# Turning q in 64x64 pieces instead of 64x128 for four of the attention groups

## The chip, the cores and the metric

The kernel runs on one NeuronCore of a Trainium2 chip. The metric is the device time of one execution in microseconds, lower is better; the time before is 195.84 us, the median of three runs.

## What is computed

Two layers in a row, on batch 8, 8 heads, 576 positions, head width 64 (so 512 columns), all inputs and the output in float32:

```python
# attention without a score matrix
q_s = softmax(q, axis=-1)            # over the 64 columns of a head
k_s = softmax(k, axis=2)             # over the 576 positions
kv  = einsum('bhsd,bhse->bhde', k_s, v)
x   = einsum('bhsd,bhde->bhse', q_s, kv)   # then heads side by side: [B, 576, 512]
# channel mix, D = 512, d_ff = 1024
x_prev = x shifted by one position, zero in front
xk = mu_k * x + (1 - mu_k) * x_prev
xr = mu_r * x + (1 - mu_r) * x_prev
k  = relu(xk @ w_k);  v = (k * k) @ w_v
out = sigmoid(xr @ w_r) * v
```

## The kernel before

**Work by group.** The attention works on 16 groups, two for each batch element b: a group (b, g) holds four heads: heads 2g and 2g+1 on partitions 0 to 63 and 64 to 127 (`r` in the code), and the heads four further on beside them in the columns (`u`). A head's 576 positions are J = 9 blocks of 64, and block j holds every ninth position. Groups (0,0) and (0,1) fold mu into the weights of X and go another way through X; they are not touched.

**Steps of a group**, by the names that the order uses (tag bg): `load` brings q, k and v by DMA; ScalarE (ACT) makes `expq`, `expk` and casts v (`cast`); VectorE (DVE) makes `rsum`, `rrec` and `scale`, which leaves the softmax of q in a tile `qs`. TensorE (PE) turns q (`T`, line 371: each 64-position block against a 64x64 identity, the result in bf16 in a PSUM pair `att_a` or `att_b`), and forms the product of k and v with the sums of k in one more column (`KV`, line 401). DVE makes the reciprocal of those sums (`rz`, line 408) and the scaled weights (`w`, line 418); ACT copies the turned q to SBUF (`qt`, line 379). Then PE multiplies both (`X`, line 541). ACT copies x out of PSUM (`xb` for the first 512 positions, `xs` for the last 64), and DVE makes the shifted copy's edge (`edge`, line 557), the difference (`diff`), the two scaled differences (`sc`, line 566) and xk and xr (`mix`, line 571).

**Blocks on PE.** For b of 1 and more one recorded operation holds several of these: `TKVbg` is T and KV, `Bbg` is the X of the group before, then T, then KV. A group in `CROSSBAR` (b of 5 and more) has its q turned by a transposing DMA and has no T. X of a few groups stands by itself (`ALONE`).

**How T is cut.** For each block of 64 positions and each half `r` of the partitions, T makes either one transpose of 64 rows by 128 columns (both `u` at once, the result on 128 PSUM partitions), or two of 64 by 64 (one for each `u`, each with its own 64 PSUM partitions). The tuple `WHOLE` lists the groups that take the first form: 18 transposes and 18 weight loads instead of 36 and 36. Before the change these are both groups of batches 0 and 1 and the first groups of batches 2 and 3. Groups (2,1), (3,1), (4,0) and (4,1) take the second form.

**Channel mix.** It runs in ten units of up to 512 positions: `k` (line 637, into PSUM banks mm_a to mm_d), `relu` on ACT, `sq` on DVE, `r` (line 673) with `th` on ACT, `v` (line 693), then `o` on DVE (line 699), which reads the bank of v and frees it, then the store.

**Order.** Nothing is scheduled at run time: the string `ORDER` lists all operations by hand-fixed name, with the buffer that each takes, and every engine runs its own in that sequence. Semaphores alone decide when. DMAs of loads and weights are issued by GpSimd (POOL) and, at the start and for stores, by SyncE (SP). The order around the change is

```
... k14 ... T of (1,0) in TKV10 -> r02 r01 r00 r03 -> B11 -> v0x -> X11 -> v0x -> k1x -> TKV20
-> r10 r11 k14 r12 r13 -> B21 -> v1x -> X21 -> v1x -> r20 -> TKV30 -> v13 -> k2x -> B31 ...
```

Of the kernel before, what the change touches and what calls it, by code (L numbers as in the profile page):

```python
# [32 lines left out]
XO = 368  # L33

FILLS = 27
WHOLE = ((0, 0), (0, 1), (1, 0), (1, 1), (2, 0), (3, 0))
FUSED = ((0, 0), (0, 1))
EARLY_UNITS = 2
SPLIT = ((1, 1),)
# [144 lines left out]
def graph(kn):  # L184
# [135 lines left out]
    def attention(b, g):  # L320
# [46 lines left out]
        def transpose_q(slot):  # L367
            for j in range(J):
                for u in ((slice(0, 128),) if (b, g) in WHOLE else two):
                    for r in range(2):  # L370
# [500 lines left out]
```

## Time and profile before

| | |
|---|---|
| median of three runs | 195.84 us (195.44 to 196.55) |
| the profiled execution | 195.36 us, of which 193.6 us are the span of the instructions |
| PE busy | 185.6 us, 96% of the span |
| DVE, ACT, POOL busy | 153.0, 138.8 and 41.4 us |
| granted TensorE clock | 0.998 on average |
| from HBM, to HBM | 33.56 MB, 9.44 MB |
| line 371 | 252 transposes (108 of 64x128, 144 of 64x64), each with a weight load, from 10.3 to 86.1 us |

Times of instructions count from the start of the span. A row of the timeline has the start, the time from there to the last end of the merged instructions, the engine, the line, the operation, its tiles as output<-inputs, and the shapes; for PE "64*128" says how many rows and columns of the array are in use. In brackets stands the idle time of the engine ahead of it and what ended it; idle times below 0.15 us are not listed. Matmuls overlap in PE's pipeline, so their starts, not their durations, show how long they hold it. Busy time of PE therefore can hide short waits.

### The profile page before, as it was taken

Reading aid. Unit: us, or ns where it says so; the run is one execution under the profiler, and the core shown is the slowest. Engines: PE = TensorE matmul, PEld = TensorE weight load, DVE = VectorE, ACT = ScalarE, POOL = GpSimd, SP = SyncE. Lnnn points to the kernel's source line nnn. Section 1 sums busy time; section 2 is a strip of 40 time slices with the busy share of each in tenths; the row PEclk is TensorE's granted clock in tenths of the full one; section 3 lists DMA queues with packets and bytes.
Section 4 is the critical chain, followed back from the end, with each engine's and each line's share of the span. In section 5 each row is a group of like instructions: output and inputs, shape, how many; then the busy total and the mean of one; then the engine's idle time right before and its main releaser. Section 6 shows DMA issues by size and latency. Waiting matters only on the chain.

```text
span 193.6 us, 4658 instructions
## 1 busy us (share of the span) xinstructions
PE 185.6 (96%) x1830; PEld 90.1 (47%) x1830; DVE 153.0 (79%) x355; ACT 138.8 (72%) x219; POOL 41.4 (21%) x65
## 2 busy tenths in 40 slices
PE   7988979999999999999999999999999999999991
PEld 2364434444535544654544444444444444444751
DVE  1899874999999999999999999988966863242531
ACT  3777999899999999898999798653754235421440
POOL 8345557554225114320210000000000000000000
PEclk9999999999999999999999999999999999999999
DMA  6999999999999999997793371449014145024813
GB/s 182 316 314 254 328 330 246 405 390 401 410 392 402 402 415 358 360 383 282 130 297 119 85 166 27 64 105 183 1 25 106 36 108 135 0 54 110 190 30 108
DMA packets 23614, 41.86 MB, mean 216 GB/s; under 512 B 9372, under 2 KB 12712, under 8 KB 23592
## 3 DMA queue, kind: packets, MB, share of 16 engines
q0 software_dynamic: 9392, 27.99, 43.9%
q1 hardware_dynamic: 13384, 12.14, 24.7%
q10 hardware_dynamic: 816, 1.44, 2.3%
q8 instruction: 14, 0.23, 0.5%
q14 instruction: 8, 0.07, 0.1%
HBM read 33.56 MB, written 9.44 MB: 222 GB/s over the span
## 4 chain that ended last, share of the span: by engine, by line
PE 84%; DMA 11%; POOL 2%; issue 0%; DVE 0%; POOLq 0%
PE mm_d L693 10%; PE mm_b L693 9%; PE mm_a L637 8%; PE mm_c L637 7%; PE mm_b L637 7%; PE mm_c L693 7%; PE mm_a L693 7%; DMA wk_ab<-in_moe_w_k_dram 7%; PE mm_d L637 6%; PE mm_c L673 5%; PE mm_d L673 5%; DMA wr<-in_moe_w_r_dram 4%; PE mm_a L673 4%; PE mm_b L673 3%; PE att_b L541 1%; PE att_a L541 1%
## 5 line engine op out<-in xcount | busy, mean ns | idle before, releaser
L693 PEld LDWEIGHTS <-k_a 128*128 128x128 bf16 x160 | 15.4, 98 | 18.5 <-issue 0.6
L673 PEld LDWEIGHTS <-xr 128*128 128x128 bf16 x144 | 13.6, 98 | 16.8 <-DMA wr<-in_moe_w_r_dram 1.5
L693 PEld LDWEIGHTS <-k_b 128*128 128x128 bf16 x136 | 12.9, 98 | 13.8 <-issue 0.4
L637 PEld LDWEIGHTS <-wk_ab 128*128 128x128 bf16 x80 | 7.8, 98 | 8.5 <-issue 0.5
L673 PE MATMUL mm_c<-wr,xr 128*128 128x512 bf16 x40 | 10.3, 380 | 1.4 <-DMA wr<-in_moe_w_r_dram 1.4
L637 PEld LDWEIGHTS <-wk_bb 128*128 128x128 bf16 x80 | 7.8, 98 | 7.7
L637 PEld LDWEIGHTS <-wk_aa 128*128 128x128 bf16 x80 | 7.6, 98 | 8.2 <-issue 0.8
L637 PEld LDWEIGHTS <-wk_ba 128*128 128x128 bf16 x80 | 7.5, 98 | 8.1 <-issue 0.5
L673 PE MATMUL mm_d<-wr,xr 128*128 128x512 bf16 x40 | 10.3, 379 | 0.0
L673 PE MATMUL mm_a<-wr,xr 128*128 128x512 bf16 x36 | 9.3, 380 | 0.0
L624 ACT ACTIVATE rel_a<-mm_b 128x512 bf16<-128x512 f32 (+1 forms) x7 | 3.6, 508 | 7.3 <-PE mm_b L637 7.1
L628 DVE TENSOR_TENSOR k_a<-rel_a 128x512 bf16<-128x512 bf16 x14 | 5.9, 421 | 3.1 <-ACT rel_a L624 2.9
L624 ACT ACTIVATE rel_c<-mm_a 128x512 bf16<-128x512 f32 (+1 forms) x11 | 6.1, 556 | 3.1 <-PE mm_a L637 2.8
L637 PE MATMUL mm_c<-xk,wk_ab 128*128 128x512 bf16 (+1 forms) x26 | 7.5, 362 | 0.6 <-ACT xk L501 0.6
L637 PE MATMUL mm_c<-xk,wk_aa 128*128 128x512 bf16 (+1 forms) x26 | 7.3, 363 | 0.0
L628 DVE TENSOR_TENSOR k_a<-rel_c 128x512 bf16<-128x512 bf16 x14 | 5.8, 417 | 1.7 <-ACT rel_c L624 1.7
L673 PE MATMUL mm_b<-wr,xr 128*128 128x512 bf16 x28 | 7.2, 379 | 0.0
L637 PE MATMUL mm_a<-xk,wk_ba 128*128 128x512 bf16 (+1 forms) x24 | 6.9, 371 | 0.0
L637 PE MATMUL mm_a<-xk,wk_bb 128*128 128x512 bf16 (+1 forms) x24 | 6.9, 370 | 0.0
L637 PE MATMUL mm_b<-xk,wk_aa 128*128 128x512 bf16 (+1 forms) x24 | 6.5, 353 | 0.0
L637 PE MATMUL mm_b<-xk,wk_ab 128*128 128x512 bf16 (+1 forms) x24 | 6.5, 352 | 0.0
L624 ACT ACTIVATE rel_a<-mm_c 128x512 bf16<-128x512 f32 x7 | 4.2, 602 | 3.2 <-PE mm_c L637 1.7
(344 smaller groups left out, 542.8 us busy)
## 6 DMA issues: line engine op xcount, KB each, us to landing
raw_k<-in_q_dram POOLq DMA_DIRECT2D x3, 576.0 KB, 8.4
raw_e<-in_k_dram POOLq DMA_DIRECT2D x3, 576.0 KB, 11.0
raw_f<-in_v_dram POOLq DMA_DIRECT2D x3, 576.0 KB, 6.5
out_dram<-th_a SPq DMA_DIRECT2D x13, 128.0 KB, 3.0
out_dram<-th_f SPq DMA_DIRECT2D x12, 128.0 KB, 2.4
out_dram<-th_b SPq DMA_DIRECT2D x10, 128.0 KB, 4.6
out_dram<-th_c SPq DMA_DIRECT2D x10, 128.0 KB, 2.4
raw_a<-in_q_dram POOLq DMA_DIRECT2D x2, 576.0 KB, 9.9
```

The lines of the kernel that those rows point to most:

```text
L541: kn.nc.tensor.matmul(kn.half(slot, u)[two[r], to:to + n], lhsT=kn.ws[w.index][two[u], r, :], rhs=x_columns(r, u, at, n), start=True, stop ...
L624: kn.nc.scalar.activation(out=kn.rels[rel.index][:, 0:n], in_=kn.bank(kf)[:, 0:n], func=ACT.Relu, scale=HALF_ROOT)
L628: kn.nc.vector.tensor_tensor(out=kn.k2s[k2.index][:, fc, 0:n], in0=kn.rels[rel.index][:, 0:n], in1=kn.rels[rel.index][:, 0:n], op=ALU.mult)
L637: kn.nc.tensor.matmul(kn.bank(kf)[:, 0:n], lhsT=kn.wk[fc // 4][ct % 2][:, ct // 2, (fc % 4) * 128: (fc % 4) * 128 + 128], rhs=kn.xs[0][:, ...
L673: kn.nc.tensor.matmul(kn.bank(rps), lhsT=kn.xs[1][:, ct, c:c + 128], rhs=kn.wr[:, ct, :], start=(ct == 0), stop=(ct == CT - 1))
L693: kn.nc.tensor.matmul(kn.bank(vps)[:, 0:width], lhsT=kn.k2s[k2.index][:, ft, 128 * m:128 * m + 128], rhs=wv_of(ft)[:, part], start=(ft == ...
```

## The change

`WHOLE` loses four groups: (1,0), (1,1), (2,0) and (3,0). Their q is turned by 36 transposes of 64x64 in place of 18 of 64x128. `ORDER` stays as it is, the other engines run the same instructions in the same sequence, and the PSUM columns and partitions that are written stay the same.

```diff
 FILLS = 27
-WHOLE = ((0, 0), (0, 1), (1, 0), (1, 1), (2, 0), (3, 0))
+WHOLE = ((0, 0), (0, 1))
 FUSED = ((0, 0), (0, 1))
```

The loop that reads it (unchanged):

```python
for j in range(J):
    for u in ((slice(0, 128),) if (b, g) in WHOLE else two):
        for r in range(2):
            kn.nc.tensor.transpose(
                out=turned(slot, r)[u, 64 * j:64 * j + 64],
                in_=kn.qss[qs.index][two[r], j, u],
                identity=kn.ident[two[r], two[r]])
```

## Prediction

> **What bounds the kernel now.** I read the page first. Its first section says that PE is busy 96% of the span, and the granted clock is 9 tenths or more in every slice:
>
> ```profile
> PE 185.6 (96%) x1830; PEld 90.1 (47%) x1830; DVE 153.0 (79%) x355; ACT 138.8 (72%) x219; POOL 41.4 (21%) x65
> ```
>
> Next the waits of PE. Five are long enough to be listed, 3.9 us together, and all lie before 27 us. The longest is the one that matters here:
>
> ```profile
> PE mm_c L673 <- DMA wr<-in_moe_w_r_dram: 1.4, 1, 1.4
> ```
>
> By these two views PE sets the end, and PE time saved after 27 us should come off the end. So I read PE's timeline at the blocks in question: first column the start, then the time until the last end, both in us. The blocks are B11 (30.48 to 31.64), TKV20 (45.43 to 46.21) and, for comparison, B21 (50.63 to 51.62), which has the 64x64 form already:
>
> ```profile
> 30.48 0.22 PE L541 MATMUL att_a<-qt_c,w_a 64*64 64x64 bf16 x4
> ...
> 30.86 0.44 PE L371 MATMUL att_a<-ident,qs_a 64*128 64x64 bf16 x18
> 31.23 0.48 PE L401 MATMUL att_a<-vv_b,ek_a 64*64 64x65 bf16 x36
> 31.64 0.60 PE L693 MATMUL mm_d<-wv_a,k_a 128*128 128x512 bf16 x2
> ...
> 45.43 0.44 PE L371 MATMUL att_a<-ident,qs_b 64*128 64x64 bf16 x18
> 45.80 0.48 PE L401 MATMUL att_a<-vv_c,ek_b 64*64 64x65 bf16 x36
> 46.21 1.04 PE L673 MATMUL mm_c<-wr,xr 128*128 128x512 bf16 x4
> ...
> 50.63 0.22 PE L541 MATMUL att_b<-qt_b,w_c 64*64 64x64 bf16 x4
> ...
> 50.90 0.48 PE L371 MATMUL att_b<-ident,qs_c 64*64 64x64 bf16 x36
> 51.20 0.49 PE L401 MATMUL att_b<-vv_a,ek_c 64*64 64x65 bf16 x36
> 51.62 0.60 PE L693 MATMUL mm_a<-wv_a,k_b 128*128 128x512 bf16 x2
> ```
>
> Starts are what counts, since matmuls overlap. 18 transposes of 64x128 hold PE for 0.37 us, 36 of 64x64 for 0.30. Twice the instructions take less time, because PE runs four 64x64 ones beside each other and two 64x128 ones (8 ns and 21 ns from start to start, on the whole).
>
> Then I asked whether PE really waits for nobody after 27 us. The list leaves out short gaps, so I read the timeline of all engines where PE reuses PSUM banks that VectorE (DVE) has to empty:
>
> ```profile
> 31.77 0.17 DVE L408 RECIPROCAL rz_a<-att_a 128x2 f32<-128x2 f32 x1 [2.35 <-PE att_a L401]
> ...
> 33.03 0.43 DVE L557 COPY xb_a<-xb_a 128x126 bf16<-128x126 bf16 x1
> ...
> 40.16 0.68 DVE L699 SCALAR_TENSOR_TENSOR th_b<-th_b,mm_d 128x512 f32<-128x512 f32 x1
> 40.33 0.59 PE L637 MATMUL mm_a<-xk,wk_ab 128*128 128x512 bf16 x2
> 40.90 0.59 PE L637 MATMUL mm_d<-xk,wk_ba 128*128 128x512 bf16 x2
> 42.02 0.67 DVE L699 SCALAR_TENSOR_TENSOR th_c<-th_c,mm_b 128x512 f32<-128x512 f32 x1
> 42.19 0.59 PE L637 MATMUL mm_c<-xk,wk_ab 128*128 128x512 bf16 x2
> 42.75 0.59 PE L637 MATMUL mm_b<-xk,wk_aa 128*128 128x512 bf16 x2
> ```
>
> Two 512-column matmuls take 0.43 us from start to start in the rows around. From 40.33 to 40.90 it is 0.57, from 42.19 to 42.75 it is 0.56. In both places PE starts 0.06 us after DVE has emptied the bank it needs (40.16 + 0.68 = 40.84, and 42.02 + 0.67 = 42.69). So PE lost 0.14 and 0.13 us to DVE, and the "busy" PE hid it. The busy time by stage (length, PE, PEld, DVE, ACT) tells who is really short:
>
> ```profile
> 24.00:33.00 9.00, 7.56 (x143) 3.76 (x142) 5.20 (x13) 9.00 (x17) 6.04 (x9) 1.00 1.18 278
> 33.00:43.00 10.00, 10.00 (x53) 4.22 (x52) 9.90 (x23) 8.71 (x12) 5.01 (x8) 1.00 1.04 395
> 43.00:62.00 19.00, 19.00 (x270) 9.13 (x269) 18.86 (x39) 18.77 (x27) 7.71 (x11) 1.00 1.04 400
> ```
>
> From 24 to 33 us ACT has no gap. From 33 to 62 us DVE has none but its own hand-overs (9.90 of 10, 18.86 of 19), and from 62 to 72 it is busy 10.00 of 10.00. PE is timed by them and is merely full as well.
>
> **The change, part by part.** Four groups get 36 transposes in place of 18, with as many weight loads. No other engine's order moves, and no wait is added. PSUM banks, columns and partitions written are the same, so the copies qt behind them cost what they do now.
>
> B11: it becomes what B21 is. From the first X matmul to the next big matmul 31.64 - 30.48 = 1.16 us now, 51.62 - 50.63 = 0.99 then: -0.17. Of this 0.11 is the step from X to T (30.86 - 30.48 = 0.38 against 50.90 - 50.63 = 0.27), since PE no longer passes from one tile shape to another there, and 0.06 the transposes.
>
> TKV20 and TKV30: no X ahead, so a shape change stays in front. Now 46.21 - 45.43 = 0.78 (TKV30: 59.02 - 58.24 = 0.78). Then 0.30 + 0.42 (T and KV in B21) = 0.72: -0.06 each. Split transposes straight behind a 128-row matmul are not in the trace. KV bounds that: straight behind a shape change it took 46.21 - 45.80 = 0.41, without one 0.42, so nothing extra; 0.05 extra is the other end (the first transposes of TKV20 behind a shape change run no slower than that). A gap of PE's own is possible too: KV of B41 took 86.60 - 86.11 = 0.49 against 0.42 in the other split blocks, with no wait shown; so +0.07 a block is the upper end. I take -0.06.
>
> TKV10: 0 at any price up to about 1.4 us, because PE waits 1.44 us behind it for the weights wr (26.93). If that cover went, it would be -0.06 as well.
>
> PE's own sum is -0.17 - 0.06 - 0.06 = -0.29 us. Now what of it reaches the end. The time that B11 gives is met at 40.90 and 42.75, where DVE decides. Would DVE be earlier? It waits 2.35 us for B11 at 31.77, but only for rz11 and w11; two squares follow, and then it stands at edge10 (33.03), which needs xs10 and xb10 from ACT. ACT starts xb10 at 31.80, straight behind th02, in its stretch without a gap, and of B11 it needs only the X matmuls ahead of T. So edge10 stays at 33.03 and so does everything that DVE does in sequence behind it: the 0.17 turns into longer waits at 40.90 and 42.75. From 42.75 on PE is where it was. TKV20 and TKV30 give 0.12 by 59 us; at 61.62 PE uses mm_b again 0.06 us after DVE is done with it (60.88 + 0.68 = 61.56), next to nothing to spare, and at 68.99 a weight load of r30 stands 0.06 us behind DVE's xr (68.18 + 0.75) and is listed with that releaser: DVE decides there too. DVE has no gap from 33.03 to there, so it cannot be earlier. After 69 us all is as before.
>
> So: -0.29 on PE, of which 0.27 to 0.29 turns into waits for DVE; change of the end 0.00, at most -0.02. The profiled execution took 195.36 us, 193.6 of it the span and 1.76 around it; it would be 195.36 again. The median of the three runs is 195.84, 0.48 above it, and that is where I put the changed kernel: **195.8 us**.
>
> One rule speaks against the change. The Trainium skill, TensorEngine Tiling (Restrictions and Gotchas), says that column tiling excludes the fast weight load, and TensorE: Matmul & The Clock Gate (LDWEIGHTS; Weight-path perf modes) gives fast loads to 128 columns alone and 1/1.2 ns per column to the others. An estimate from the second page is 53 ns for each 64-column load, 1.9 us for 36 if they come one after another, some +1.5 us in each of TKV20 and TKV30. The sum by it would be +3.0, so 198.8. The trace agrees that these loads are longer (108 ns on average against 95 for the 64x128 ones at L371) and disagrees that this costs anything in B21, where 36 loads and transposes pass in 0.30 us.
>
> **The rivals.**
> 1. *PE's gain reaches the end*: -0.29, so 195.55. For it: PE 96% and the chain of waits, which is PE from 26.93 on. Against it: the two gaps above and a DVE without gaps. It would still be within 0.5%, which is 0.98 us and about what a measurement of this kernel can tell from no change.
> 2. *Slower: the weight loads stand in a row*. The place is T20 and T30, where no X has put PE into the 64x64 shape. If the loads there came one by one at the 108 ns that L371's 64x64 loads last, T would take 36 x 0.108 = 3.9 us in place of 0.37, both together +7.0, so 202.8; PE would pass DVE as the bound, as there is no more than some 0.04 us of waiting to eat up behind them. It decides from (0.98 + 0.12 + 0.04)/72 = 16 ns extra for each transpose, 24 ns in place of 8. Against it: 8 ns in all four split blocks of this trace (B21, B31, B40, B41), though each has an X ahead.
> 3. *Slower by little*: PE's own gaps of 0.07 in three blocks, +0.2 less the gain; nothing visible, within 0.5%.
> That the change does not do what it says is no rival: the built program has four runs of 18 more transposes and nothing else.
>
> **How the numbers follow.** Forecast (DVE takes the gain) 0.62; rival 1 0.15; rival 3 0.06; all three within 0.5%, 0.83. Rival 2 past its point 0.09, and 0.03 for the spread of the runs (195.44 to 196.55 is 0.57% alone): slower 0.12. Faster by over 0.98 us has no mechanism, since even the whole of PE's sum is 0.29; 0.05 for the spread and what I do not see. The range goes from the lowest run less rival 1, 195.44 - 0.29 = 195.15, to the highest run, 196.6; only rival 2 and the far ends lie outside.
>
> **What would show it.** Right: T at B11, TKV20, TKV30 with x36 and 0.30 us to KV; B11 0.99 us long; the gap at 40.90 about 0.14 longer or the wait at 42.75 in its place; DVE's edge10 at 33.03 and all PE starts after 69 us where they are now. Wrong: PE starts after 69 us earlier by 0.1 or more (rival 1: then DVE had room that I did not see); T20 or T30 longer than 0.45 us (rival 2); a DVE instruction between 33 and 69 us that moves.

## The result: slower, by a pause inside one block

| | before | changed |
|---|---|---|
| median | 195.25 us (195.0 to 197.28) | 196.41 us (195.93 to 197.91) |
| ratio | 1 | 1.0065, 95% interval 1.005 to 1.008 |
| profiled execution | 195.36 us, span 193.6 | 196.10 us, span 194.2 |

Both medians are of 18 runs taken beside each other, so the loss is 196.41 - 195.25 = 1.16 us. The median of before that the prediction used, 195.84, was that of three of these runs, and lies 0.59 us above that of all 18.

The page of the changed kernel:

```profile
PE 185.5 (95%) x1902; PEld 90.1 (46%) x1902; DVE 152.9 (79%) x355; ACT 138.7 (71%) x219; POOL 41.4 (21%) x65
...
q8 instruction: 15, 0.25, 0.5%
```

144 more instructions on PE (72 matmuls, 72 weight loads), and PE busy no longer than it was (185.5 against 185.6 us). The loss is therefore idle time of PE. Its list of waits has a row of a kind that before did not have in this stage, "issue", which means that PE waited for no semaphore that the profile shows:

```profile
PE mm_c L673 <- DMA wr<-in_moe_w_r_dram: 1.3, 1, 1.3
...
PE att_b L401 <- issue: 0.6, 1, 0.6
```

PE's timeline of the changed kernel (start, time to the last end) at the blocks that the prediction named, then at B40, the block of group (4,0), whose own instructions the change does not touch:

```profile
30.29 0.22 PE L541 MATMUL att_a<-qt_c,w_a 64*64 64x64 bf16 x4
...
31.27 0.60 PE L693 MATMUL mm_d<-wv_a,k_a 128*128 128x512 bf16 x2
...
39.12 0.38 PE L637 MATMUL mm_c<-xk,wk_ab 128*128 128x512 bf16 x1
39.48 0.59 PE L637 MATMUL mm_a<-xk,wk_aa 128*128 128x512 bf16 x2
40.13 0.59 PE L637 MATMUL mm_a<-xk,wk_ab 128*128 128x512 bf16 x2
40.73 0.59 PE L637 MATMUL mm_d<-xk,wk_ba 128*128 128x512 bf16 x2
...
42.02 0.59 PE L637 MATMUL mm_c<-xk,wk_ab 128*128 128x512 bf16 x2
42.58 0.59 PE L637 MATMUL mm_b<-xk,wk_aa 128*128 128x512 bf16 x2
...
45.26 0.48 PE L371 MATMUL att_a<-ident,qs_b 64*64 64x64 bf16 x36
45.57 0.47 PE L401 MATMUL att_a<-vv_c,ek_b 64*64 64x65 bf16 x36
45.97 1.04 PE L673 MATMUL mm_c<-wr,xr 128*128 128x512 bf16 x4
...
60.88 0.59 PE L637 MATMUL mm_a<-xk,wk_ab 128*128 128x512 bf16 x2
61.44 0.59 PE L637 MATMUL mm_b<-xk,wk_aa 128*128 128x512 bf16 x2
...
70.51 0.22 PE L541 MATMUL att_b<-qt_b,w_c 64*64 64x64 bf16 x4
...
70.78 0.48 PE L371 MATMUL att_b<-ident,qs_c 64*64 64x64 bf16 x36
71.08 0.45 PE L401 MATMUL att_b<-vv_a,ek_c 64*64 64x65 bf16 x31
72.16 0.23 PE L401 MATMUL att_b<-vv_a,ek_c 64*64 64x65 bf16 x5 [0.64 <-issue]
72.32 1.04 PE L673 MATMUL mm_a<-wr,xr 128*128 128x512 bf16 x4
```

VectorE's rows in the same trace, just ahead of three of these places:

```profile
32.95 0.35 DVE L557 COPY xb_a<-xb_a 128x126 bf16<-128x126 bf16 x1 [0.38 <-ACT xb_a L552]
38.76 0.67 DVE L699 SCALAR_TENSOR_TENSOR th_a<-th_a,mm_a 128x512 f32<-128x512 f32 x1
60.71 0.67 DVE L699 SCALAR_TENSOR_TENSOR th_b<-th_b,mm_b 128x512 f32<-128x512 f32 x1
```

And the rows of before that belong beside them, at mm_b near 61 us and at KV of B40:

```profile
61.19 0.59 PE L637 MATMUL mm_a<-xk,wk_ab 128*128 128x512 bf16 x2
61.62 0.59 PE L637 MATMUL mm_b<-xk,wk_aa 128*128 128x512 bf16 x2
...
71.17 0.49 PE L401 MATMUL att_b<-vv_a,ek_c 64*64 64x65 bf16 x36
```

Three readings. First, the parts that were changed did what was forecast: B11 takes 31.27 - 30.29 = 0.98 us, TKV20 45.97 - 45.26 = 0.71. Second, VectorE took the gain: a matmul that used to follow after 0.22 us starts 0.36 us after the one before it at 39.48, the gap at 40.73 is 0.60, and at 61.44 there is one of 0.56 where before had 0.43. At 39.48 and 61.44 PE starts 0.05 and 0.06 us after VectorE has emptied the bank that it needs (38.76 + 0.67 = 39.43, and 60.71 + 0.67 = 61.38). Third, in KV of B40 the 32nd of 36 matmuls does not come. The 31st starts at 71.33, the next at 72.16: a pause of 0.83 us in the middle of a row of equal instructions, none of which waits for a semaphore. Before has the 36 in one row.

### The profile page after: what moved, and what is told of

It is laid out like the page before. It is cut to its first block, busy times and chain, and to the rows that moved or that the text cites. A ratio compares the mean times of both kernels' runs of the same rounds, so it can differ in the third digit from the quotient of the medians.

```text
span 194.2 us, 4802 instructions
## 1 busy us (share of the span) xinstructions
PE 185.5 (95%) x1902; PEld 90.1 (46%) x1902; DVE 152.9 (79%) x355; ACT 138.7 (71%) x219; POOL 41.4 (21%) x65
## 3 DMA queue, kind: packets, MB, share of 16 engines
q10 hardware_dynamic: 816, 1.44, 2.3%
## 4 chain that ended last, share of the span: by engine, by line
PE 84%; DMA 11%; POOL 2%; issue 1%; DVE 0%; POOLq 0%
PE mm_d L693 10%; PE mm_b L693 9%; PE mm_a L637 8%; PE mm_c L637 7%; PE mm_b L637 7%; PE mm_c L693 7%; PE mm_a L693 7%; DMA wk_ab<-in_moe_w_k_dram 7%; PE mm_d L637 6%; PE mm_c L673 5%; PE mm_d L673 4%; DMA wr<-in_moe_w_r_dram 4%; PE mm_a L673 4%; PE mm_b L673 3%; PE att_b L541 1%; PE att_a L541 1%
```

## What the pause is: theories

The page counts DMA packets by queue. The instruction queue q8 carries 14 packets of 16384 bytes before and 15 now, with PE's own instructions up from 3671 to 3815 recorded ones. The line of before:

```profile
q8 instruction: 14, 0.23, 0.5%
```

In the trace's packets one of them lies just ahead of the pause: it starts at 69.68 us and lands at 70.78. The DMA view of that stretch alone has it:

```profile
q8 instruction: 1, 0.02, 5.8%
```

**Theory 1 (pages).** PE's program comes in pages by DMA. PE has passed the last instruction of one page and the next is not usable yet. In the changed kernel a pause of 0.56 us also ends at 16.82 (hidden, since PE waits for wr later), and between it and the pause in B40 PE ran 767 matmuls with their weight loads, 1535 instructions with one that only waits: six times 256, but for one. So a page is taken to be 256 instructions, and counting on in steps of 256 gives every other border. The two pauses end 1.27 and 1.38 us after a page has landed. In this stage a page's transfer starts 2.15 to 3.58 us after PE has reached the border before it, 3.29 us after for this one. (Elsewhere in the runs some start as much as 1.8 us ahead of that border.) Two borders that PE reaches 4.94 us apart (66.39 us in B31, 71.33 in B40) are then too close: 3.29 to the start, 1.10 to land, 1.38 to be used make 5.77, and 5.77 - 4.94 = 0.83. This sum splits the measured time into its parts; it must come out, and tests nothing. The experiments have to. The Trainium skill, Runtime: NRT & Kernel Launch (Instruction fetch mechanics), says that the program is refilled in blocks of 16 KiB, 256 instructions, and that crossing a border costs one tail-bump, "mostly hidden"; the trace agrees with the size, and here the cost is not hidden.

By this theory nothing is wrong with split transposes. They only add 144 instructions ahead of B40, so every border behind them falls 144 instructions earlier in the work. Before, the same stretch had its borders at 63.13 (among big matmuls), 70.94 and 83.93.

**Theory 2 (cost of each split T).** The four groups cost about 0.3 us each somewhere (their loads, shape changes, or a late effect of them).

A further question: did VectorE really take PE's gain, as forecast?

## The experiments

Ratios are to the kernel before on the same chip, with their 95% intervals; "border" is a border of 256 PE instructions.

**1. One group fewer, (3,0).**
```diff
-WHOLE = ((0, 0), (0, 1))
+WHOLE = ((0, 0), (0, 1), (3, 0))
```


> The changed kernel with group (3,0) left at 18 transposes of 64x128; (1,0), (1,1) and (2,0) split. Theory 1 (PE's program comes in pages of 16384 B, 256 instructions; the page border that falls into KV of block B40 comes only 5 us after the border before it, and the page is not there yet): 36 instructions fewer ahead of B40 move that border behind the block, to a matmul near 74 us, 7.7 us after the border before. No pause in B40 (KV there 0.29 to 0.35 us from first to last start, not 1.1); time ratio to before 0.998 to 1.002. Theory 2 (each split T costs by itself, 0.3 us a group): three quarters of the loss stay, ratio 1.004 to 1.006.

Measured 1.0017 (1.0006 to 1.0029), and no pause in B40:

```profile
71.31 0.49 PE L401 MATMUL att_b<-vv_a,ek_c 64*64 64x65 bf16 x36
```

Three of four splits are in, and three quarters of the loss are not. The page that was late now lands 3.18 us ahead of its border, which PE reaches at 74.55.

**2. One group fewer, (1,0)**, the one whose T lies under the wait for wr.
```diff
+WHOLE = ((0, 0), (0, 1), (1, 0))
```


> The changed kernel with group (1,0) left at 18 transposes of 64x128; (1,1), (2,0) and (3,0) split. Theory 1 (pages): the number of PE instructions ahead of B40 is the same as with (3,0) left whole, so the border falls behind B40 again: no pause there, ratio 0.998 to 1.002, although another group is the one left whole. Theory 2 (cost of each split T): T of (1,0) is covered by PE's wait for wr, so leaving it whole gives nothing back: ratio 1.006.

Measured 1.0014 (0.9995 to 1.0033); KV of B40 again 36 in one row. Which group stays whole does not matter for the pause, only the count. Theory 2 at 0.3 us a group falls with these two: from the first r matmul behind wr to the last matmul of the kernel the two profiles need 162.48 and 162.45 us, before 162.48. The ratios of experiments 1, 2 and 4 (1.0014 to 1.0019, two of the intervals wholly above 1) leave 0.3 us or so that these stretches do not show in 1 and 2; that rest is open.

**3. Before, with 72 idle pairs.** An idle pair is a weight load and a matmul on zeros, whose result nobody reads. No T is changed.
```diff
+    pad_slot = Slot("mm")
+...
+        for i in range(72):
+            kn.nc.tensor.matmul(kn.bank(pad_slot)[two[i % 2], 0:64], lhsT=kn.still[0:64, 0:64],
+                                rhs=kn.still[0:64, 64:128], start=True, stop=True)
```

(In place of "..." stands the head of the function; `ORDER` has the operation as `pad:2`, just ahead of r02, in PSUM bank mm_c.)

> The kernel before, all its T as they were, with 72 pairs of a 64x64 weight load and a 64-column matmul on a zeroed tile put in front of r02, where PE waits 1.4 us for the weights wr: the same 144 PE instructions more as in the change, none of them a transpose, and about 1 us of PE time that the wait covers. Theory 1 (pages): the borders stand at B31 and B40 exactly as in the changed kernel, so KV of B40 pauses by 0.5 to 1.2 us and the ratio is 1.003 to 1.007. Theory 2 (cost of each split T): no T is split, ratio 0.999 to 1.001.

Measured 1.0079 (1.0065 to 1.0094), a little above the expected end. The pause sits behind the same instruction, the 31st matmul of KV in B40:

```profile
71.36 0.45 PE L411 MATMUL att_b<-vv_a,ek_c 64*64 64x65 bf16 x31
72.74 0.23 PE L411 MATMUL att_b<-vv_a,ek_c 64*64 64x65 bf16 x5 [0.93 <-issue]
```

(Lines are ten further on.) The page had landed at 71.38, 1.36 us before PE went on. The loss of the change is here without the change.

**4. Another block made shorter: (4,0) whole, all four splits in.**
```diff
+WHOLE = ((0, 0), (0, 1), (4, 0))
```


> The changed kernel, all four groups split, with group (4,0), which was split before as well, turned by 18 transposes of 64x128. Theory 1 (pages): block B40 is 36 instructions shorter, the border that fell into it comes after it: no pause; the whole T costs PE 0.16 us in that block. Ratio 0.999 to 1.002. Theory 2 (cost of each split T, as in the change): the four splits stay, ratio 1.005 to 1.008.

Measured 1.0019 (1.0007 to 1.003). B40 has no pause. KV of TKV20 and TKV30 took 0.11 us longer than in the changed kernel, by a pause of 0.12 and 0.11 us at no border; why is open.

**5 and 6. Less DMA traffic.** The changed kernel and the one before, with the loads of q, k and v of batches 4 to 7 cut to 64 of 576 columns. Both kernels leave out the rest of that input and compute on old data. (At the second "..." the destination of the load is narrowed in the same way.)
```diff
+        n_cols = 64 if b >= 4 else J * D
 ...
-                             ap=[[J * D, 128], [4 * S * D, u.stop - u.start], [1, J * D]])
+                             ap=[[J * D, 128], [4 * S * D, u.stop - u.start], [1, n_cols]])
 ...
```


> The changed kernel, with the loads of q, k and v of batches 4 to 7 cut to 64 of the 576 columns of each row (the rest of the raw tiles keeps old data; it leaves out eight ninths of that input). PE's instructions and the page borders are those of the changed kernel. Theory 1 with a late page (the page is late because its transfer starts 3.3 us after it is due, behind the input loads that keep the DMA engines full until 76 us): the transfer now starts within 1.5 us of the border in B31, and KV of B40 has no pause (0.29 to 0.35 us). Theory 1 without that part (the page is late for another reason, its own length or PE's speed): the pause of 0.5 us or more stays. Theory 2 (cost of each split T): 1.0 us more than the kernel before with the same cut loads.

> The kernel before with the same cut loads (it leaves out eight ninths of q, k and v of batches 4 to 7), to set beside the changed kernel with cut loads. Theory 1 with a late page: the same time as that one within 0.3 us. Theory 2: 1.0 us less than that one. Both theories: 0.1 to 1 us faster than the kernel before, since a few waits for loads near 36 to 39 us go.

The busy times from 66.4 to 71.4 us, last three columns granted clock, DMA share and GB/s, of the changed kernel and then of the one with cut loads:

```profile
66.40:71.40 5.00, 5.00 (x150) 2.74 (x136) 5.00 (x13) 5.00 (x9) 0.83 (x2) 1.00 1.04 406
```

```profile
66.40:71.40 5.00, 5.00 (x160) 2.78 (x144) 5.00 (x13) 5.00 (x9) 0.86 (x2) 1.00 0.44 105
```

With cut loads the page started 2.14 us after the border in B31 in place of 3.29 (the expected 1.5 was missed), landed 1.83 us ahead of the next border, and there was no pause in B40:

```profile
71.10 0.49 PE L403 MATMUL att_b<-vv_a,ek_c 64*64 64x65 bf16 x36
```

Changed 195.35 us (ratio 1.0008, 0.9999 to 1.0017), before 195.23 (0.9998, 0.9989 to 1.0007): the loss of 1.16 us shrinks to 0.12 with all four splits in. That less traffic would also speed up the kernel before was wrong. So the pause needs both: two borders 5 us apart, and a transfer that starts late, as it does here with the DMA engines full. Full engines alone do not say how late: before has borders at 45.53 and 51.34 us, 5.81 apart, and the page for the second starts 1.46 us after the first, at the same DMA share of 1.04. What else sets the start is open.

**7. 54 pairs in place of 72.**

> The kernel before with 54 pairs of a weight load and a 64-column matmul ahead of r02, in place of the 72 that gave 1.0079: 108 instructions more ahead of B40 instead of 144. Theory 1 (pages): the border of 256 falls behind B40, near 74 us, so no pause there, ratio 0.999 to 1.002. A theory by which the added PE work itself (or its place) costs the time: three quarters of the 72 pairs' loss, ratio 1.006.

Measured 1.0004 (0.9993 to 1.0015), no pause in B40. 18 pairs more, in PE time that a wait covers, make the difference between 1.0004 and 1.0079. The pairs themselves cost nothing.

**8. The change and 56 pairs: a whole page more.**

> The changed kernel with 56 pairs of a weight load and a 64-column matmul ahead of r02: 144 + 112 = 256 instructions more than before ahead of B31 and B40, one whole page, so that from there on the borders stand where they stand in the kernel before. Theory 1 (pages): no pause in B40, although more instructions are added than in the change; a border comes into B11 near 31 us instead, 4.5 us after the one before, and may pause there by up to 0.5 us, of which the waits for VectorE at 40.9 and 42.8 us take up most. Ratio 0.999 to 1.003. A theory by which more PE instructions cost more: ratio 1.008 or more.

Measured 1.0036 (1.0022 to 1.005), above the expected range. B40 has its 36 in one row again, as expected with 256 instructions more. But a border that I had not counted as close now falls at the end of B21, 5.7 us after the one in TKV20:

```profile
51.19 0.48 PE L411 MATMUL att_b<-vv_a,ek_c 64*64 64x65 bf16 x35
52.01 0.19 PE L411 MATMUL att_b<-vv_a,ek_c 64*64 64x65 bf16 x1 [0.35 <-issue]
```

Its page started 3.67 us after the border before it and landed at 50.62, 1.39 us before PE went on. The border expected in B11 gave a pause of 0.17 us from start to start (31.18 to 31.35), 1.44 us after its page had landed. Counted from the border at 16.6 us, the two pauses stand 511 and 1023 instructions on, two and four times 256 but for one, as in the changed kernel. The theory held, my use of it did not: I had taken the start of the transfer at about 2 us there.

**9 and 10. The changed kernel twice more**, one profile each.

> The changed kernel once more, for a second profile: the length of the pause in KV of B40 against the span. Theory 1 (pages): the page's transfer starts when the DMA engines let it, so the pause differs from run to run (0.5 to 1.5 us), always after the 31st of the 36 matmuls, and the span differs by as much (193.4 us and the pause, within 0.4).

> The changed kernel a third time, for a third profile, expected as the second: the pause after the 31st matmul of KV in B40, 0.5 to 1.5 us, and a span of 193.4 us and the pause, within 0.4.

Pauses of 1.05 and 1.08 us, again after the 31st matmul; spans 194.55 and 194.64. That is 193.4 and the pause, within 0.2. From the first r matmul behind wr to the last matmul it is 162.48 us before, and 163.33, 163.50 and 163.53 in the three profiles of the change: +0.85, +1.02 and +1.05. The medians differ by 1.16; the rest lies within what the start of that r matmul (26.6 to 27.5 us in these profiles) and a longer pause in some runs can make, and was not separated.

**11 and 12. Four sums of VectorE left out.**
```diff
+            if b in (2, 3):
+                return None
             return kn.nc.vector.reduce_sum(...)
```
once in the kernel before, once in that with (1,1), (2,0) and (3,0) split.

> The kernel before without the four row sums of q on VectorE for batches 2 and 3 (left out: rsum of b = 2 and 3; old sums are used instead), 1.3 us each between 40 and 66 us. If VectorE decides PE's times from 33 to 69 us, its waits at 42.8 and 61.6 us go and the kernel is faster by 0.1 to 0.3 us (ratio 0.998 to 1.000); if PE alone decides, nothing moves.

> The same four row sums left out, with groups (1,1), (2,0) and (3,0) split and (1,0) left whole (no page border in B40). PE gains 0.16 + 0.07 + 0.07 = 0.30 us in these blocks. If VectorE took that gain in the kernels with the sums, it now comes through from 42 us on: the 0.16 of B11 is still met at 40.9 us, the 0.14 of the two others shows at the end against the kernel before without the sums (0.0007 less in the ratio, 0.1 to 0.2 us in the spans, counted from the first r matmul). If the gain is lost elsewhere, the two are equal.

Ratios 0.9999 (0.999 to 1.0008) and 0.9995 (0.9987 to 1.0004): these intervals tell nothing apart. From the first r matmul to the last matmul it is 162.35 and 162.19 us, 0.16 less, where with the sums it is 162.48 and 162.45, 0.03 less. But 0.11 of the 0.16 is a pause in KV of B41 that the first of these kernels has and the second has not (0.41 against 0.30 us from first to last start). At KV of B40, 0.06 of the expected 0.14 had come through (44.09 and 44.03 us after the first r matmul). Inconclusive: VectorE still held PE up at 39 to 41 us in both, before the sums that were left out.

## Why the prediction was wrong, point by point

The measured 196.41 us lies inside the stated 195.15 to 196.6, and that is luck: the range stood around a median of before that was 0.59 us too high, and its upper end was the highest of three runs. What was forecast is no change, and the kernel became 1.16 us slower, clear of the noise. The chance given to a loss of more than 0.5% (0.12) stood for rival 2 and the spread of the runs, and neither is the cause.

- **PE's sum (-0.17, -0.06, -0.06): right.** B11 0.98 us (0.99 forecast), TKV20 and TKV30 0.71 each (0.72). Split transposes straight behind a shape change, not in the trace of before, cost nothing extra: T to KV 0.31 us. The weight loads did not come in a row (rival 2), and the estimate of +1.5 us in each of TKV20 and TKV30 did not come either.
- **TKV10 covered by wr: right.** PE waited 1.29 us behind it.
- **VectorE takes the gain: right in cause and size, and only in part in its place.** New waiting of PE in the changed kernel, read as start to start beyond the usual: 0.14 at 39.48, 0.03 more at 40.73, 0.13 at 61.44, together 0.30 for a gain of 0.30. The first of these is one bank earlier (mm_a) than the two places that were named, 40.90 and 42.75; at the second of them nothing was added (42.58 - 42.02 = 0.56, as before). edge10 on VectorE waits 0.38 us for ACT, as forecast (32.95 us, 6.2 after the first r matmul; before 6.1). B40 begins 43.8 us after the first r matmul, before 43.7; a short pause of 0.1 us in KV of B31 is of that size. Rival 1 is out: the kernels of experiments 1 and 2 have most of PE's gain and no pause, and need 162.48 and 162.45 us from the first r matmul to the last matmul, before 162.48. The test by leaving out sums did not settle how much would come through if VectorE were free.
- **"After 69 us all is as before": the step that failed.** It rested on "no wait is added", and looked for waits among semaphores, buffers and neighbouring engines. The instructions themselves arrive by DMA, and 144 more of them move the borders at which they must have arrived. The term for it in the sum was "a gap of PE's own", +0.07 a block at most, taken from one row (B41, 0.49 against 0.42), +0.2 in all, with a chance of 0.06 (rival 3) and within 0.5%. It measured 0.83, 1.05 and 1.08 us in a single block, one that was not changed. So rival 3 had the right sign (slower, by a gap of PE's own), the wrong size and the wrong place, and nothing of the cause; and the bound was no bound, since the row it came from shows a short pause of another kind, at no border.
- **What could have been read.** The page of before has "q8 instruction: 14" packets, and the trace has their times. They show starts of 0.7 to 4.9 us after the border ahead of them while the DMA engines are full, and 1.33 us between a landing and the use of its page at 16.35 us. Setting the borders 144 instructions earlier in the work puts two of them into B31 and B40, 4.86 us apart by the timeline of before. An estimate from rows of before: with the 3.52 us to the start that the page behind 51.34 us took, 3.52 + 1.10 + 1.33 = 5.95, a pause of some 1.1 us; with the 1.46 us of the page ahead of it, none. The place and the risk could have been read, the size could not.

## What to carry to other kernels

When an edit adds or removes instructions on an engine whose queue of work is dense, count the instructions ahead of each dense stretch in steps of 256 and look where the borders fall. In three kernels here, two borders that PE reached 4.9 to 5.9 us apart, with the DMA engines full, paused it though no wait was added; where the transfer started 1.5 or 2.1 us after the first border there was no pause. A loss in a block that the edit did not touch, marked "issue" and always behind the same instruction, is the sign; to test it, change the count by a few dozen instructions that cost nothing before blaming the edit.

## What the runs showed that I had not expected

- The pages for which PE paused in B11, B21 and B40 took 1.0 to 1.2 us to land, PE went on 1.35 to 1.44 us after that, and their transfers began 3.3 to 3.7 us after the border before with the DMA engines full (2.14 at a DMA share of 0.44, where there was no pause).
- PE ran through its 64x64 blocks at 8 ns for each pair of weight load and matmul. An estimate from this: 256 instructions can pass in little over 1 us; among 512-column matmuls, 0.216 us from start to start, the same 256 take some 28 us.
- Short pauses of 0.06 to 0.12 us turn up in KV mostly at places that are no borders (B41 before, B31 in the changed kernel; in experiment 2 one stands three matmuls behind a border). Their cause stays open.
